# VectorE in source order inside each of the first 48 steps, weight conversion two chunks further ahead

## The chip, the cores and the metric

One core of a Trainium2 chip runs the whole program. The metric is the device time of one execution in microseconds (us), the median of three runs.

## What is computed

Three stages run one after the other on 1536 tokens (2 batches of 768) of width 512, all in float32 at the interface.

```
x = attention(q, k, v)          # 8 heads of 64; each query sees keys within 16 places,
                                # and the 24 block summaries (max of k, mean of v)
h = x @ w_in                    # 512 -> 2048
g = h * tanh(log1p(exp(h)))     # "mish"
x = g @ w_out                   # 2048 -> 512
out = x                         # then, where x @ w_skip > 0:
out += gate * relu(x @ w1[e]) @ w2[e]   # e = argmax of x @ w_gate, 8 experts of 512 -> 1024 -> 512
```

## The kernel before, in words

The change touches the middle stage, the two dense products around mish. Its tokens are cut into 4 blocks of 384 (`BLK`), its inner width of 2048 into 16 chunks f of 128. One **step** i is one pair (block n, chunk f), and there are 64 steps. Their order is the list `seq`: steps 0 to 9 are block 0 with f = 0 to 9, steps 10 to 25 are block 1 with f = 0 to 15, steps 26 to 31 finish block 0 with f = 10 to 15, and blocks 2 and 3 follow with 16 steps each. So the first 48 steps are blocks 0, 1 and 2.

Step i traces in the loop of `blocks()`, in this order:

- `m1` (L298): 12 matmuls on TensorE make h, the hidden chunk of 128 x 384, from the transposed tokens xt and the weights w. Each float32 operand is held as a high and a low part, so each product takes three matmuls. h lies in a pool of two PSUM buffers.
- `s1` (L311) on VectorE cuts h off at 20 and ScalarE (L312) takes exp.
- `s3` and `s4` of the step before: L331 and L335 on VectorE, then g is split in a high part on ScalarE (L339) and a low part on GpSimd (L340).
- `s2` and `s2b` of this step: L318 on VectorE, two activations on ScalarE (L319, L320), L326 on VectorE (the last reader of h), L327 on GpSimd.
- `more_w`: weight chunks are converted up to the number that `wneed` gives for this half step.
- the attention, loading and routing work that a table has set for half step 2i (`run_half`).
- `m2` of step i-2 (L369): 9 matmuls add g times the second weight into three PSUM tiles of 128 x 512.
- `more_w` and `run_half` again, for half step 2i+1.

In the texts m1(i), s1(i), s2(i), s2b(i), s3(i), s4(i) and m2(i) mean that function's work for step i. On VectorE s1, s2, s2b, s3 and s4 are one instruction each.

**Conversion.** The dense weights arrive as float64 words of 64 bits, in 32 chunks: chunk 2f holds the first weight of f, which m1 needs, chunk 2f+1 the second one, which m2 needs. `split_w` makes two float32 parts of one: three integer instructions on VectorE (L180, L182, L183), a copy on ScalarE (L186) that is the high part, and a subtraction on GpSimd (L187) that is the low one. Chunks 0 to 3 are converted in the start-up. After that `wneed(h)` says how many have to be done by half step h: h + 3 in the first 20 half steps, later one for every 2.5 half steps. Raw chunks are loaded `LA` = 6 chunks before their conversion.

**Attention** is cut in units of 128 queries by 4 heads, six to a block: units 0 to 5 for block 0 run in the start-up, units 6 to 11 for block 1 in steps 0 to 8. Each has four parts, `att_a` (scores, maximum, exp), `att_b` (transposes), `att_c` (product with v, division) and `att_d` (transposes on TensorE, L282; the high part of xt on ScalarE, L286; the low part on VectorE, L287). `AO[n]` gives the half steps of the four parts, counted from the unit's first. xt(u) is the VectorE instruction at L287 for unit u; m1(10), the first of block 1, needs xt(11).

**Order.** The program is traced in the order above, but the instructions of each engine are put in order by the tile framework, which picks among what is ready on a timeline of its own. `tc.manual_schedule` keeps the traced order for the engines that it is given. Before the change it stands around the start-up (SyncE alone) and around the expert stage (all engines); in the 64 steps every engine's order is picked.

```
def wneed(h):
    if h < 2 * FS:
        return h + 3
    return min(2 * NCH, max(2 * FS + 3, int(2 * FS + WC + (h - 2 * FS) * WD)))
```

Of the kernel before, what the change touches and what calls it, by code (L numbers as in the profile page):

```python
# [25 lines left out]
NCH = DFF // 128  # L26
# [14 lines left out]
WD = 0.4  # L41
AB = (0, 0, 42, 62)
AS = (0, 1.5, 2, 4)
AO = ((), (0, 3, 6, 8), (0, 5, 8, 11), (0, 5, 8, 11))
SH = 6
SI = 6
MPS = (6, 7, 8, 9, 10, 11)
# [4 lines left out]
GB = 5  # L52
XL = 2
LA = 6
LOADS = ("k0 q0 k1 c1 c0 q2 v0 q1 q4 v2 n1 n0 k2 v4 n2 v5 k3 q3 v3 q5 W4 v1").split()
STEPS = ("e0 e3 K0 x0 e2 z14 a0 e4 x4 w2 e1 K1 a4 x2 a2 z4 z8 b2 x3 V z8 x1 b0 y0 y4 b4 e5 c0 y2 c4 y5 c2 a1 "
         "a3 x5 d2 z4 y3 a5 d0 w1 d4 z4 y1 b1 b3 b5 c1 c3 c5 w4 d1 d3 w3 z4 d5").split()
# [3 lines left out]
def body(ctx: ExitStack, tc: tile.TileContext, a):  # L61
# [64 lines left out]
    def ones_v(t):  # L126
        for s in range(2):
            G.memset(t[96 * s:96 * s + 24, s, :, 64:65], 32.0)
# [162 lines left out]
    def m1(n, f):  # L291
        w = ring_t[f]
        x = xt[n]
        h = psh.tile([128, BLK], F32, tag="h", name="h")
        c = 0
        for k in range(4):
            for wi, xi in ((0, 0), (0, 1), (1, 0)):
                T.matmul(out=h, lhsT=w[wi][:, k * 128:(k + 1) * 128], rhs=x[:, xi, k, :],  # L298
                         start=(c == 0), stop=(c == 11))
                c += 1  # L300
        g_t[n, f] = [h]
# [3 lines left out]
    def s1(n, f, c=ALL):  # L305
        h = g_t[n, f][0]
        if c.start == 0:
            u = ep.tile([128, BLK], F32, tag="u", name="u")
            g_t[n, f] = [h, u, None, None, None]
        u = g_t[n, f][1]  # L310
        V.tensor_scalar(out=u[:, c], in0=h[:, c], scalar1=20.0, scalar2=None, op0=ALU.min)  # L311
        A.activation(out=u[:, c], in_=u[:, c], func=AF.Exp)  # L312
# [16 lines left out]
    def s3(n, f, c=ALL):  # L329
        h, u, nn = g_t[n, f][0:3]  # L330
        V.scalar_tensor_tensor(out=nn[:, c], in0=nn[:, c], scalar=2.0, in1=u[:, c], op0=ALU.add, op1=ALU.mult)  # L331
# [457 lines left out]
    def load_w(n):  # L789
        while wn[0] < min(n, 2 * NCH):  # L790
            f, c = wq[wn[0]]
            if f < NR:
                raw = ring.tile([128, 512], I64, tag="w", name="rawr")
            else:
                raw = stg.tile([128, 512], I64, tag="stg", name="raw")
            st["sp"] = nc.sync.dma_start(out=raw, in_=a["wio"][f, c]).ins
            st["w", f, c] = raw
            wn[0] += 1

    def more_w(n):  # L800
        while wn[1] < min(n, 2 * NCH):
            k = wn[1]
            load_w(min(k + LA - k % 2, 2 * NR) if k < 2 * NR - 1 else max(2 * NR, k + 2))
            split_w(*wq[k])
            wn[1] += 1
# [67 lines left out]
    def startup():  # L873
# [10 lines left out]
        for p in range(2):  # L884
            ones_v(vw[p])
        for x in LOADS:
            ITEMS[x[0]](int(x[1:]))
# [10 lines left out]
    def at_half(h, fn, x):  # L898
        half.setdefault(h, []).append((fn, x))

    seq = ([(0, f) for f in range(FS)] + [(1, f) for f in range(NCH)] + [(0, f) for f in range(FS, NCH)] +
           [(n, f) for n in range(2, NBLK) for f in range(NCH)])
    for n in range(1, NBLK):
        for x in range(6):
            u = 6 * n + x
            for o, fn in zip(AO[n], (att_a, att_b, att_c, att_d)):
                at_half(int(AB[n] + AS[n] * x) + o, fn, u)
# [30 lines left out]
    def run_half(h):  # L938
        for fn, x in half.pop(h, []):
            if fn in (kload, tri_load):  # L940
                with tc.issue_after(st["sp"]):
                    fn(x)
            else:
                fn(x)

    def wneed(h):
        if h < 2 * FS:
            return h + 3
        return min(2 * NCH, max(2 * FS + 3, int(2 * FS + WC + (h - 2 * FS) * WD)))

    rawp = gp = None

    def blocks():
        nonlocal rawp, gp
        last = len(seq) - 1
        for i in range(len(seq)):
            if i == 3 * NCH:
                att.close()
                rawp = ctx.enter_context(tc.tile_pool(name="rawp", bufs=4))
                gp = ctx.enter_context(tc.tile_pool(name="gp", bufs=2))  # L960
            m1(*seq[i])
            if i < last:
                s1(*seq[i])
            if i >= 1:
                s3(*seq[i - 1])
                s4(*seq[i - 1])
            if i < last:
                s2(*seq[i])
                s2b(*seq[i])
            more_w(wneed(2 * i))  # L970
            run_half(2 * i)
            if i >= 2:
                n, f = seq[i - 2]
                m2(n, f)
                if m2_ends(n, f)[1]:
                    for t in range(3):
                        if f == NCH - 1:
                            ev(3 * n + t)
                        else:
                            ev_part(t)  # L980
            more_w(wneed(2 * i + 1))
            if i >= 3 * NCH + 2:
                load_e(min(NRAW, 2 * (i - 3 * NCH)))
            run_half(2 * i + 1)
        cs = [slice(128 * t, 128 * t + 128) for t in range(3)]
        for t in range(3):
            for fn in (s1, s2, s2b, s3, s4):
# [128 lines left out]
```

## Time and profile before

| what | value |
|---|---|
| median of 3 runs | 594.76 us (594.69 to 595.54) |
| the profiled execution, its own time | 595.44 us |
| its span, first to last instruction | 593.5 us |
| TensorE busy | 522.0 us (88%) |
| VectorE busy | 428.7 us (72%) |
| ScalarE busy | 288.5 us (49%) |
| GpSimd busy | 300.7 us (51%) |
| mean granted TensorE clock | 0.970 |

The profiled execution took 595.44 us, 0.68 us more than the median; 1.9 us of it lie outside the span. All times in the rows are counted from the start of the span. In the profile's lines PE is TensorE's matmuls, PEld its weight loads, DVE VectorE, ACT ScalarE, POOL GpSimd, SP SyncE. A row of a timeline gives the start, the length, the engine, the line and what is written and read; "x12" after it means twelve instructions merged in one row; the bracket is the engine's idle time just before and what ended it. The share of busy time is a mean over stages with different limits, so stretches have to be read apart.

### The profile page before, as it was taken

To read this page: it belongs to the slowest core of one execution; us is meant where nothing else is said; L and a number is where in the kernel's file an instruction comes from. 1 tells how busy PE (TensorE), PEld (TensorE's weight loads), DVE (VectorE), ACT (ScalarE), POOL (GpSimd) and SP (SyncE) were. 2 spreads that over 40 slices of the span, in tenths; PEclk is the share of its full clock that TensorE was granted. 3 is DMA by queue.
4 is the path that set the end of the run, shared out by engine and by line. 5 is a ranking of instruction groups with operands and counts; after the bars stand their busy time and mean duration, and the time that the engine had idled before them with its cause. 6 is when DMAs were issued, how large, how long until landed. Compare 5 with 4: busy or idle time off the path is not lost. (4 is left out here: it accounts for less than half of the span.)

```text
span 593.5 us, 11154 instructions
## 1 busy us (share of the span) xinstructions
PE 522.0 (88%) x3870; PEld 424.1 (71%) x3870; DVE 428.7 (72%) x904; ACT 288.5 (49%) x602; POOL 300.7 (51%) x334
## 2 busy tenths in 40 slices
PE   4498798678999999999999999999879979598994
PEld 2266566567778888898888889888547857386883
DVE  2447999999998677677798896797587257466314
ACT  1545655445665446445444454434436247366322
POOL 3223365574787554436445454454457256666403
PEclk8599999979999999999999999999999999799999
DMA  8916444845320023250100317630229369891100
GB/s 263 334 33 236 150 150 159 283 152 177 111 61 28 7 55 122 76 180 19 48 14 2 142 48 276 222 129 1 107 81 353 140 230 397 300 359 49 35 19 15
DMA packets 40614, 82.57 MB, mean 139 GB/s; under 512 B 4749, under 2 KB 17297, under 8 KB 40536
## 3 DMA queue, kind: packets, MB, share of 16 engines
q1 hardware_dynamic: 38280, 75.03, 37.5%
q0 software_dynamic: 2256, 6.57, 3.5%
q8 instruction: 39, 0.64, 0.5%
q14 instruction: 39, 0.32, 0.2%
HBM read 72.92 MB, written 9.44 MB: 139 GB/s over the span
## 5 line engine op out<-in xcount | busy, mean ns | idle before, releaser
L298 PE MATMUL h<-xt,w 128*128 128x384 f32 x768 | 157.4, 347 | 10.3 <-DVE hn L326 5.1
L369 PE MATMUL o<-w,g 128*128 128x512 f32 x576 | 152.8, 404 | 7.6 <-ACT g L339 6.5
L298 PEld LDWEIGHTS h<-xt,w 128*128 128x128 f32 x768 | 134.1, 190 | 19.1 <-DVE hn L326 7.5
L369 PEld LDWEIGHTS o<-w,g 128*128 128x128 f32 x576 | 104.6, 189 | 32.8 <-ACT g L339 9.9
L327 POOL TENSOR_TENSOR hn<-hn,u 128x384 f32<-128x384 f32 (+1 forms) x66 | 79.8, 1209 | 81.7 <-ACT u L320 36.7
L340 POOL TENSOR_TENSOR g<-hn,g 128x384 fp32r<-128x384 f32 (+1 forms) x66 | 68.6, 1041 | 67.4 <-ACT g L339 63.7
L550 POOL TENSOR_TENSOR hl<-rawe,hl 128x128 fp32r<-128x128 f32 (+1 forms) x64 | 56.1, 902 | 17.7 <-ACT hl L546 17.0
L339 ACT ACTIVATE g<-hn 128x384 fp32r<-128x384 f32 (+1 forms) x66 | 33.9, 514 | 63.6 <-DVE hn L335 58.5
L319 ACT ACTIVATE u<-nn,two 128x384 f32<-128x384 f32 (+1 forms) x66 | 39.8, 604 | 47.6 <-DVE nn L318 47.6
L187 POOL TENSOR_TENSOR w<-r,w 128x512 fp32r<-128x512 f32 x32 | 44.1, 1382 | 30.1 <-ACT w L186 29.8
L335 DVE SCALAR_TENSOR_TENSOR hn<-nn,hn 128x384 f32<-128x384 f32 (+1 forms) x66 | 48.0, 729 | 14.9 <-POOL hn L327 14.7
L550 DVE TENSOR_TENSOR hl<-rawe,hl 128x384 fp32r<-128x384 f32 (+1 forms) x64 | 43.6, 719 | 17.5 <-ACT hl L546 15.8
L331 DVE SCALAR_TENSOR_TENSOR nn<-nn,u 128x384 f32<-128x384 f32 (+1 forms) x66 | 46.2, 701 | 13.2 <-ACT u L320 13.0
L318 DVE SCALAR_TENSOR_TENSOR nn<-u 128x384 f32<-128x384 f32 (+1 forms) x66 | 46.2, 700 | 12.0 <-ACT u L312 11.9
L312 ACT ACTIVATE u<-u 128x384 f32<-128x384 f32 (+1 forms) x66 | 33.9, 513 | 33.6 <-DVE u L311 32.0
L546 ACT ACTIVATE hl<-rawe 128x512 fp32r<-128x512 f32 (+1 forms) x64 | 43.1, 729 | 13.7 <-PEq L734 5.2
L585 PE MATMUL p<-hl,slx 128*128 128x512 f32 x168 | 41.7, 397 | 2.5 <-ACT slx L563 2.0
L602 PE MATMUL po<-hl,slh 128*128 128x512 f32 x168 | 43.1, 399 | 0.0
L585 PEld LDWEIGHTS p<-hl,slx 128*128 128x128 f32 x168 | 30.7, 188 | 9.4 <-ACT slx L563 2.7
L311 DVE TENSOR_SCALAR u<-h 128x384 f32<-128x384 f32 (+1 forms) x66 | 35.3, 535 | 2.6 <-PE h L298 2.6
L326 DVE TENSOR_TENSOR hn<-nn,h 128x384 f32<-128x384 f32 (+1 forms) x66 | 35.2, 534 | 1.4
L602 PEld LDWEIGHTS po<-hl,slh 128*128 128x128 f32 x168 | 30.6, 188 | 6.1
(173 smaller groups left out, 742.9 us busy)
## 6 DMA issues: line engine op xcount, KB each, us to landing
rawe<-w SPq DMA_DIRECT2D x64, 512.0 KB, 6.0
rawr<-wio SPq DMA_DIRECT2D x30, 512.0 KB, 5.1
vw<-vx SPq DMA_DIRECT2D x40, 97.5 KB, 2.1
xs<-x SPq DMA_DIRECT2D x12, 256.0 KB, 3.2
out<-x SPq DMA_DIRECT2D x12, 256.0 KB, 2.4
kw<-kx SPq DMA_DIRECT2D x18, 160.0 KB, 3.2
q<-qx SPq DMA_DIRECT2D x20, 128.0 KB, 2.8
kt<-kt SPq DMA_DIRECT2D x4, 384.0 KB, 4.9
```

What stands on the lines that cost most here:

```text
L187: G.tensor_tensor(out=w[1][:, o:o + 512], in0=r, in1=w[0][:, o:o + 512].bitcast(F32), op=ALU.subtract)
L298: T.matmul(out=h, lhsT=w[wi][:, k * 128:(k + 1) * 128], rhs=x[:, xi, k, :], start=(c == 0), stop=(c == 11))
L318: V.scalar_tensor_tensor(out=nn[:, c], in0=u[:, c], scalar=2.0, in1=u[:, c], op0=ALU.add, op1=ALU.mult)
L327: G.tensor_tensor(out=hn[:, c], in0=hn[:, c], in1=u[:, c], op=ALU.mult)
L331: V.scalar_tensor_tensor(out=nn[:, c], in0=nn[:, c], scalar=2.0, in1=u[:, c], op0=ALU.add, op1=ALU.mult)
L335: V.scalar_tensor_tensor(out=hn[:, c], in0=nn[:, c], scalar=2.0, in1=hn[:, c], op0=ALU.subtract, op1=ALU.mult)
L340: G.tensor_tensor(out=g[:, 1, c], in0=hn[:, c], in1=g[:, 0, c].bitcast(F32), op=ALU.subtract)
L369: T.matmul(out=o_t[t], lhsT=g[:, gi, t * 128:(t + 1) * 128], rhs=w[wi][:, 512:1024], start=(first and i == 0), stop=(end and i == 2))
L546: A.activation(out=w[0][:, c], in_=r[:, c], func=AF.Copy)
L550: eng.tensor_tensor(out=w[1][:, d], in0=r[:, d], in1=w[0][:, d].bitcast(F32), op=ALU.subtract)
L585: T.matmul(out=ps, lhsT=x[:, xi + k, :], rhs=w[wi][:, 512 * half:512 * half + 512], start=(k == 0 and xi == 0 and wi == 0), stop=(k == 3 a ...
L602: T.matmul(out=ps, lhsT=hs[f // 4][:, xi + f % 4, :], rhs=w[wi][:, 512 * (f % 2):512 * (f % 2) + 512], start=(f == 0 and i == 0), stop=(f ...
```

## The change

Three edits. `AO[1]` sets part d of units 6 to 11 one half step earlier (7 for 8). `wneed` asks for two more chunks in the first 20 half steps. And each of the first 48 steps runs inside a `manual_schedule` for VectorE. Lines of the code behind the insertion move down by one (L311 becomes L312), inside and behind the loop by more.

```
-AO = ((), (0, 3, 6, 8), (0, 5, 8, 11), (0, 5, 8, 11))
+AO = ((), (0, 3, 6, 7), (0, 5, 8, 11), (0, 5, 8, 11))
...
+MAN = {mybir.EngineType.DVE}
...
     def wneed(h):
         if h < 2 * FS:
-            return h + 3
+            return h + 5
...
-        for i in range(len(seq)):
+        def step(i):
+            nonlocal rawp, gp
             if i == 3 * NCH:
...
             run_half(2 * i + 1)
+
+        for i in range(len(seq)):
+            with (tc.manual_schedule(engines=MAN) if i < 3 * NCH else ExitStack()):
+                step(i)
```

What it does to the order of instructions shows in the lists of the two built programs. In the new VectorE list the instructions of one step stand in traced order, but each step has a context of its own, and those of two neighbouring steps are still mixed.

**VectorE, from the last instruction of the start-up into steps 0 and 1.** h, u, nn and hn are the tiles of s1, s2 and s2b; bits, r and rawr those of a chunk's conversion; mx and psc belong to att_a. Before:

```order
L287 TENSOR_TENSOR xt_487<-psx_642,xt_487 128x2x128
L180 TENSOR_SCALAR bits_748<-rawr_258 128x512
L182 SCALAR_TENSOR_TENSOR bits_748<-rawr_258,bits_748 128x512
L214 TENSOR_REDUCE mx_683<-psc_672 128x4
L183 SCALAR_TENSOR_TENSOR r_749<-rawr_258,bits_748 128x512
L215 TENSOR_SCALAR mx_683<-mx_683 128x4
L180 TENSOR_SCALAR bits_755<-rawr_260 128x512
L182 SCALAR_TENSOR_TENSOR bits_755<-rawr_260,bits_755 128x512
L183 SCALAR_TENSOR_TENSOR r_756<-rawr_260,bits_755 128x512
L311 TENSOR_SCALAR u_662<-h_649 128x384
```

With the change:

```order
L288 TENSOR_TENSOR xt_487<-psx_642,xt_487 128x2x128
L312 TENSOR_SCALAR u_664<-h_651 128x384
L312 TENSOR_SCALAR u_752<-h_739 128x384
L319 SCALAR_TENSOR_TENSOR nn_667<-u_664 128x384
L327 TENSOR_TENSOR hn_671<-nn_667,h_651 128x384
L181 TENSOR_SCALAR bits_680<-rawr_258 128x512
L183 SCALAR_TENSOR_TENSOR bits_680<-rawr_258,bits_680 128x512
L332 SCALAR_TENSOR_TENSOR nn_667<-nn_667,u_664 128x384
L184 SCALAR_TENSOR_TENSOR r_681<-rawr_258,bits_680 128x512
```

Before, chunks 4 and 5 and one maximum of att_a stand ahead of s1(0). Now s1(0) and s1(1) stand first, and chunk 4 follows s2b(0).

**VectorE, the ten instructions that end with s4(9).** ksum and sl belong to the key summaries of the second batch. s4(9) is the last row of both lists. Before:

```order
L182 SCALAR_TENSOR_TENSOR bits_1736<-rawr_1445,bits_1736 128x512
L180 TENSOR_SCALAR bits_1794<-rawr_1447 128x512
L326 TENSOR_TENSOR hn_1442<-nn_1438,h_1417 128x384
L156 TENSOR_REDUCE ksum10_105<-sl_1638 128x24
L318 SCALAR_TENSOR_TENSOR nn_1495<-u_1487 128x384
L156 TENSOR_REDUCE ksum10_105<-sl_1650 128x24
L182 SCALAR_TENSOR_TENSOR bits_1794<-rawr_1447,bits_1794 128x512
L331 SCALAR_TENSOR_TENSOR nn_1438<-nn_1438,u_1430 128x384
L326 TENSOR_TENSOR hn_1499<-nn_1495,h_1474 128x384
L335 SCALAR_TENSOR_TENSOR hn_1442<-nn_1438,hn_1442 128x384
```

With the change:

```order
L319 SCALAR_TENSOR_TENSOR nn_1487<-u_1479 128x384
L184 SCALAR_TENSOR_TENSOR r_1441<-rawr_1272,bits_1440 128x512
L181 TENSOR_SCALAR bits_1456<-rawr_1274 128x512
L327 TENSOR_TENSOR hn_1491<-nn_1487,h_1466 128x384
L181 TENSOR_SCALAR bits_1500<-rawr_1369 128x512
L183 SCALAR_TENSOR_TENSOR bits_1456<-rawr_1274,bits_1456 128x512
L332 SCALAR_TENSOR_TENSOR nn_1487<-nn_1487,u_1479 128x384
L183 SCALAR_TENSOR_TENSOR bits_1500<-rawr_1369,bits_1500 128x512
L184 SCALAR_TENSOR_TENSOR r_1457<-rawr_1274,bits_1456 128x512
L336 SCALAR_TENSOR_TENSOR hn_1491<-nn_1487,hn_1491 128x384
```

In the first piece pieces of chunks 24 and 25, two summaries, s2(10) and s2b(10) stand ahead of s4(9). In the second it is chunks 20, 21 and 22, and no summary and nothing of step 10. Counted from the top of the list, s4(9) is instruction 203 of VectorE before and 192 now. The eleven that have gone behind it are L180 and L182 of chunks 23, 24 and 25, L183 of chunk 22, two summaries (L156), s2(10) and s2b(10). Nothing has come ahead of it.

**VectorE and TensorE around xt(11), with the change.** xn_1336 is unit 11's attention output, psx_1382 its transpose. VectorE:

```order
L336 SCALAR_TENSOR_TENSOR hn_1366<-nn_1362,hn_1366 128x384
L319 SCALAR_TENSOR_TENSOR nn_1427<-u_1419 128x384
L184 SCALAR_TENSOR_TENSOR r_1376<-rawr_1179,bits_1375 128x512
L263 RECIPROCAL rs_1333<-rs_1333 128x4
L327 TENSOR_TENSOR hn_1431<-nn_1427,h_1406 128x384
L272 TENSOR_TENSOR xn_1336<-psv_1322,rs_1333 128x256
L288 TENSOR_TENSOR xt_1010<-psx_1382,xt_1010 128x2x128
```

TensorE, the last three of the nine matmuls of m2(7), two of m1(9), six of m1(10) and the transpose:

```order
L370 MATMUL o_887<-w0_1183,g_1424 128x512
L370 MATMUL o_888<-w0_1183,g_1424 128x512
L370 MATMUL o_889<-w0_1183,g_1424 128x512
L299 MATMUL h_1466<-xt_487,w0_1373 128x384 x2
L299 MATMUL h_1526<-xt_1010,w0_262 128x384 x2
L299 MATMUL h_1526<-xt_1010,w1_263 128x384
L299 MATMUL h_1526<-xt_1010,w0_262 128x384 x2
L299 MATMUL h_1526<-xt_1010,w1_263 128x384
L283 MATMUL psx_1382<-cb_94,xn_1336 128x128 x2
```

Before, xn(11) and xt(11) have four other VectorE instructions between them, and on TensorE the transpose follows m1(7). Now xt(11) stands directly behind xn(11), and the transpose behind m2(7), two matmuls of m1(9) and six of m1(10).

## Rows read from the trace of the kernel before

**Rows 1.** Stretches: length, then PE, PEld, DVE, ACT, POOL busy, clock, DMA share, GB/s.

```profile
45.00:60.00 15.00, 12.36 (x126) 9.04 (x126) 11.28 (x26) 7.57 (x23) 4.25 (x4) 1.00 0.68 243
60.00:105.00 45.00, 37.45 (x287) 28.40 (x288) 43.69 (x84) 26.96 (x64) 25.27 (x21) 1.00 0.49 151
105.00:135.00 30.00, 21.52 (x102) 17.29 (x102) 30.00 (x57) 13.74 (x26) 19.15 (x16) 0.89 0.58 207
135.00:150.00 15.00, 12.78 (x72) 11.03 (x74) 13.89 (x22) 8.07 (x18) 7.78 (x8) 1.00 0.58 176
150.00:200.00 50.00, 49.03 (x328) 39.79 (x321) 46.53 (x80) 29.96 (x61) 36.49 (x31) 1.00 0.21 61
200.00:250.00 50.00, 50.00 (x344) 43.36 (x342) 35.93 (x73) 27.44 (x55) 25.48 (x22) 1.00 0.25 72
```

**Rows 2.** VectorE's lines in 54.5 to 138 us: busy us, mean ns, idle before.

```profile
L182 DVE SCALAR_TENSOR_TENSOR bits<-rawr,bits 128x512 int32<-128x512 int32 x22 | 15.0, 683 | 0.1
L180 DVE TENSOR_SCALAR bits<-rawr 128x512 int32<-128x512 int32 x22 | 14.9, 683 | 1.1 <-ACT sc L217 0.6 <-ACT at L245 0.4
L183 DVE SCALAR_TENSOR_TENSOR r<-rawr,bits 128x512 int32<-128x512 int32 x19 | 12.8, 676 | 0.1
L318 DVE SCALAR_TENSOR_TENSOR nn<-u 128x384 f32<-128x384 f32 x11 | 9.0, 822 | 0.1
L335 DVE SCALAR_TENSOR_TENSOR hn<-nn,hn 128x384 f32<-128x384 f32 x9 | 8.3, 926 | 0.1
...
L326 DVE TENSOR_TENSOR hn<-nn,h 128x384 f32<-128x384 f32 x11 | 6.0, 541 | 0.0
...
L156 DVE TENSOR_REDUCE ksum<-sl 128x24 f32<-128x768 f32 x2 | 1.9, 940 | 0.0
```

**Rows 3.** Timeline of TensorE and VectorE at the end of the start-up.

```profile
53.98 0.96 PE L298 MATMUL h<-xt,w 128*128 128x384 f32 x4
...
54.10 0.42 DVE L287 TENSOR_TENSOR xt<-psx,xt 128x256 fp32r<-128x256 f32 x1 [0.97 <-ACT xt L286]
...
57.99 1.33 PE L298 MATMUL h<-xt,w 128*128 128x384 f32 x6
...
59.31 0.55 DVE L311 TENSOR_SCALAR u<-h 128x384 f32<-128x384 f32 x1
```

**Rows 4.** Timeline of 111 to 122 us, all engines.

```profile
111.77 0.41 PE L282 MATMUL psx<-cb,xn 128*128 128x128 f32 x2 [1.14 <-DVE xn L271]
...
112.22 0.39 ACT L286 ACTIVATE xt<-psx 128x256 fp32r<-128x256 f32 x1 [0.37 <-PE psx L282]
...
120.27 0.68 DVE L180 TENSOR_SCALAR bits<-rawr 128x512 int32<-128x512 int32 x1
...
120.86 0.67 DVE L183 SCALAR_TENSOR_TENSOR r<-rawr,bits 128x512 int32<-128x512 int32 x1
...
121.53 3.57 PE L298 MATMUL h<-xt,w 128*128 128x384 f32 x10 [2.08 <-POOL w L187]
```

**Rows 5.** The view of Rows 1, one short stretch.

```profile
120.00:125.00 5.00, 3.47 (x11) 3.48 (x12) 5.00 (x8) 2.18 (x4) 3.15 (x3) 0.55 0.39 148
```

**Rows 6.** Timeline from s4(9) to m1(15), TensorE, ScalarE, GpSimd and VectorE.

```profile
138.03 0.55 DVE L335 SCALAR_TENSOR_TENSOR hn<-nn,hn 128x384 f32<-128x384 f32 x1
...
138.67 0.53 ACT L339 ACTIVATE g<-hn 128x384 fp32r<-128x384 f32 x1 [1.48 <-DVE hn L335]
...
139.42 1.02 POOL L340 TENSOR_TENSOR g<-hn,g 128x384 fp32r<-128x384 f32 x1
...
143.33 2.35 PE L369 MATMUL o<-w,g 128*128 128x512 f32 x9 [0.70 <-ACT x L352]
...
145.52 4.35 PE L298 MATMUL h<-xt,w 128*128 128x384 f32 x24
...
149.80 0.85 PE L138 MATMUL psv<-vl,strip 128*24 128x128 f32 x22
...
157.26 4.45 PE L298 MATMUL h<-xt,w 128*128 128x384 f32 x24
```

## Prediction

> **What bounds the kernel now.** I first read the busy time of each engine by stretches [rows 1], because the shares over the whole span mix stages with different limits. From 200 us on TensorE is busy 50.00 us of 50 and VectorE only 35.9: there the order of VectorE's instructions can cost something, but it can hardly gain. Between 60 and 135 us it is the other way round. VectorE is busy 43.69 of 45 and 30.00 of 30 us, and TensorE loses 7.6 us in the first of these stretches and 8.5 in the second; from 135 to 150 us it loses 2.2, from 150 to 200 us 1.0. So VectorE sets the pace in steps 0 to about 11, and TensorE from about step 13 to the end of the dense stage. A better order can give back at most what TensorE lost there.
>
> Next I read what VectorE does in its own stretch [rows 2]. Of its time, 15.0, 14.9 and 12.8 us go into conversion, and there is hardly an idle moment: 1.1 us ahead of L180, ended by ScalarE. A conversion instruction of 0.68 us starts 0.59 us after the one before it [rows 4], so one costs some 0.08 us less than its mean length says. With that, L180, L182 and L183 cost 0.60 each, s2 0.74, s2b 0.47, a summary (L156) 0.86.
>
> So the question is what stands in VectorE's list ahead of the instructions that TensorE waits for. The best mark is s4(9), which starts at 138.03 us [rows 6]: with it m2(9) becomes possible, and soon after TensorE works without a gap to speak of.
>
> **What leaves the place ahead of s4(9).** By the lists, s4(9) is VectorE's instruction 203 before and 192 now. Eleven have gone behind it: seven of conversion (7 x 0.60 = 4.2 us), two summaries (1.7), s2(10) and s2b(10) (1.2). Nothing has come ahead of it. That is **-7.1 us**, as long as VectorE stays busy. The two more chunks of the new `wneed` are no load here: before, the planner had run even further ahead, into chunk 25, by itself. What is moved costs the same later: ahead of s4(17) the new list is 23 instructions shorter, ahead of s4(25) only four, and from 150 us on TensorE sets the pace. Chunk 31 now stands just ahead of s4(25), whose m2(25) is the first to need it.
>
> **What it costs in waiting.** VectorE works strictly along its list. Where conversion used to fill a wait, now there may be nothing.
>
> - *Start.* xt(5) ends at 54.52 us [rows 3]. Before, chunks 4 and 5 and a maximum follow at once and s1(0) comes at 59.31. Now s1(0) and s1(1) follow, and s1(1) needs the end of m1(1). Of m1(0) and m1(1) twelve matmuls are left by then, at 0.18 us each (24 in 4.35 us) [rows 6], so 2.2 us and a little for the last to end: s1(1) starts at about 57.0. Less the 0.5 us of s1(0), VectorE idles **2.0 us**.
> - *xt(11).* It now stands directly behind xn(11), and its transpose stands on TensorE behind m2(7) and eight matmuls of m1. From the end of s4(7): high part of g 0.53 and low part 1.02 [rows 6], of m2(7) then seven matmuls at 0.26 (9 in 2.35 us) 1.8, eight at 0.18 1.4, the transposes 0.41 and ScalarE's part 0.39 [rows 4]: 5.6 us. VectorE meanwhile has s2(8), one L183, s2b(8), a reciprocal and xn(11). The last two, which have no row here, I put at 0.5 together by their few columns; in all 2.3 us. So it waits **3.3 us**, and s1(9) and all behind it wait too.
> - *s1(5) and s1(8).* Here the new TensorE list has six matmuls of m2(i-2) inside m1(i), so s1(i) closes a ring: s4(i-2), both parts of g (1.55), four m2 (1.0), ten m1 (1.8), 4.4 us. VectorE has by the prices above about 4.2 and 4.0 us of work in between: **0.6 us** in all. At the other steps the ring has a microsecond or more of room.
>
> Together 5.9 us, so s4(9) comes 1.2 us earlier and ends at 137.4.
>
> **From there to the end.** TensorE gets the high part of g(9) at 138.0. From there to m1(15) its new list holds m1(12), m1(13), m1(14) (36 x 0.18 = 6.5 us) and m2(9), m2(10), m2(11) with six matmuls of m2(12) (33 x 0.26 = 8.6): 15.1 us, and I add 1.0 us for places where it still waits for s4(10) and s2b(11), which gain less than s4(9). m1(15) then starts at 154.1. Before, it starts at 157.26 [rows 6], with three matmuls of m2(12) (0.8) and 24 small ones of the value summaries (22 take 0.85) [rows 6] more behind it, so the like point is 155.6. The gain is 1.5 us. The 1.1 us that VectorE idled ahead of L180 [rows 2] was a conversion standing in line for a PSUM buffer that an exp of att_a still read. Now conversion and attention follow each other as traced, and I take it as gained, with a little for the row's waits behind it: **-2.7 us** in all. From m1(15) on TensorE has the same work as before and is full; routing and the later attention are moved by some places on VectorE, under TensorE's 50.00 of 50, and I cost that at nothing. If this cover fails, it costs what s4 comes late, in steps 40 to 43 above all, where 26 small routing instructions stand in two steps.
>
> The other two edits go into the same lists: `AO` moves xt(6) to xt(11) half a step earlier in the traced order, and the raw chunks are loaded six chunks ahead as before. In rows 2 no conversion waits for a load, so I cost the loads at nothing, between nothing and the 0.6 us of one instruction.
>
> The sum is made against the profiled execution (595.44 us, which is 0.68 above the median); I set it on the median: 594.76 - 2.7 = **592.0 us**. The bounds of this case itself: the start wait is at best 1.4 us (s1(0) filled in) and the wait at xt(11) is halved if the low part of g comes early, which gives 2.5 us more, 589.5; with no gain from the 1.1 us and each wait half as long again, 594.6.
>
> **Rivals.**
>
> *A, the waits don't come.* The whole 7.1 us arrive, and 1.0 that TensorE lost after 150 us: 586.7 us. For it: TensorE loses 19 us from 60 to 150 us, so there is room [rows 1]. Against it: the lists show the wait at xt(11) plainly.
>
> *B, the clock.* Before, the granted clock falls to a mean of 0.55 between 120 and 125 us [rows 5], a mix of 2.4 and 1.2 GHz, after TensorE had stood still for 2.08 us ahead of m1(9) [rows 4]; ten of that step's matmuls then took 3.57 us, 1.8 more than at 0.18 each. That was hidden behind VectorE. Now m1(9) and m1(10) stand ahead of xt(11), so it would be seen: 593.8 us. Against it: with attention and m2 spread more evenly, TensorE's gaps should be shorter. The Trainium skill (TensorE: Matmul & The Clock Gate, What's actually happening) says that a gate sets the array's clock by how busy it has lately been; by that rule the wait at xt(11), in which TensorE is working, would not bring the fall, and the gap ahead of m1(9) would.
>
> *C, slower: VectorE stands in line.* In the old list a late operand held up one instruction, and conversion ran on. In the new one all of s3, s4, s2 stand behind it, and TensorE behind them. The place is the ring at s1(5), s1(8) and xt(11), with under half a microsecond of room at the first two. It runs through GpSimd's low part of g, and GpSimd also makes the low part of each chunk, for which TensorE stood 2.08 us before m1(9) [rows 4]. If it comes in between at all three, 6.2 us are lost: 594.76 - 2.7 + 6.2 = 598.3 us. It decides from two such delays on. For it: s1(5) and s1(8) have no slack. Against it: GpSimd is busy only 25.3 of 45 us [rows 1].
>
> A price that also belongs here: s2 and s4 take 822 and 926 ns while s2b, with as many elements, takes 541 [rows 2]. If the ten s2 of steps 0 to 9 came to s4's price, 1.0 us would be lost, which stays inside the range. The Trainium skill (GPSIMD Engine Reference, Specifications) says that GpSimd shares its SBUF interfaces with VectorE and that instructions with two SBUF inputs contend; s2 and s4 read two from SBUF, s2b one, so the rows agree. By that rule s2, s3 and s4, which now stand closer together, could meet GpSimd more often.
>
> That the change does nothing is excluded by the lists; that it keeps a single traced order is not what it does, since two steps are still mixed.
>
> **How the numbers follow.** The forecast has 0.48, A 0.18, B 0.14, C 0.20. A measurement of this kernel can tell about 0.2% from no change, 1.2 us. The forecast is faster by more than that in about six parts of seven, A always, B in a third, C never, with a mild form near zero: **faster 0.63, same 0.19, slower 0.18**. The range that leaves out 0.2 reaches to A on one side and to a C with one and a half of its three delays on the other (592.0 + 3.1, and the contention's 1.0): **586.5 to 596.2**. The forecast's own is 589.5 to 594.6.
>
> **What would show it.** Right: VectorE idle for about 2 us at 55 to 57 us, by m1, and 3 us ahead of an L288 near 121 us; s4(9) between 135 and 138 us and no L157 ahead of it; TensorE's lost time from 105 to 150 us down from 10.7 to about 7 us, and a clock near 1.00 from 120 to 135. Wrong: idle time of VectorE ahead of L312 that adds up to over 8 us (C), a clock under 0.9 there (B), a wait at xt(11) under 1 us (A), or TensorE under 49 us in 50 after 200 us, by which the cost that I put at nothing would be real.

## The result, and the profile after

The changed kernel takes **603.09 us** (median of 4 runs, 601.01 to 607.12) against 594.73 us (4 runs, 594.35 to 595.54) of the kernel before: 1.0136 times as long, with a 95% interval of 1.0100 to 1.0173. It is slower by about 8 us, where 592.0 us was predicted with a range of 586.5 to 596.2. The profiled execution took 603.09 us, its span is 601.2 us, the mean granted clock 0.956. Executions more than 1.5% above the fastest one of their kernel are left out of every ratio below.

The stretches after, in the columns of [rows 1]: length, then busy time of PE, PEld, DVE, ACT and POOL, clock, DMA share, GB/s.

```profile
60.00:105.00 45.00, 37.06 (x262) 28.77 (x262) 43.41 (x78) 25.47 (x60) 23.97 (x21) 0.92 0.54 167
105.00:135.00 30.00, 21.42 (x136) 17.43 (x135) 25.35 (x51) 12.10 (x24) 13.68 (x12) 0.94 0.55 191
135.00:150.00 15.00, 11.27 (x44) 8.84 (x44) 14.69 (x22) 7.50 (x15) 11.31 (x10) 0.89 0.24 78
150.00:200.00 50.00, 48.50 (x289) 41.90 (x289) 44.48 (x78) 27.43 (x61) 30.96 (x28) 1.00 0.29 90
200.00:250.00 50.00, 48.69 (x374) 41.50 (x373) 42.14 (x82) 28.29 (x57) 29.31 (x27) 1.00 0.30 87
250.00:300.00 50.00, 50.00 (x369) 44.30 (x368) 31.83 (x71) 24.36 (x48) 21.15 (x20) 1.00 0.26 79
350.00:400.00 50.00, 47.56 (x247) 42.99 (x246) 39.69 (x101) 22.04 (x43) 21.81 (x19) 0.93 0.58 191
```

From 105 to 135 us VectorE has 4.65 us in which it does nothing, where before it had none [rows 1], and TensorE is busy no longer for it (21.42 us, before 21.52). From 200 to 250 us TensorE loses 1.3 us, which it did not before.

Two kinds of loss show in VectorE's lines from 55.5 to 142.2 us, the stretch that answers to [rows 2]: busy us, mean ns, idle before.

```profile
L183 DVE SCALAR_TENSOR_TENSOR bits<-rawr,bits 128x512 int32<-128x512 int32 x19 | 12.9, 687 | 0.2
L181 DVE TENSOR_SCALAR bits<-rawr 128x512 int32<-128x512 int32 x19 | 12.7, 682 | 0.0
L184 DVE SCALAR_TENSOR_TENSOR r<-rawr,bits 128x512 int32<-128x512 int32 x18 | 12.1, 679 | 0.2
L319 DVE SCALAR_TENSOR_TENSOR nn<-u 128x384 f32<-128x384 f32 x10 | 8.6, 864 | 0.2 <-ACT u L313 0.2
L336 DVE SCALAR_TENSOR_TENSOR hn<-nn,hn 128x384 f32<-128x384 f32 x9 | 8.5, 940 | 0.1
L332 DVE SCALAR_TENSOR_TENSOR nn<-nn,u 128x384 f32<-128x384 f32 x10 | 8.3, 830 | 0.0
L312 DVE TENSOR_SCALAR u<-h 128x384 f32<-128x384 f32 x11 | 6.1, 552 | 3.0 <-PE h L299 3.0
...
L288 DVE TENSOR_TENSOR xt<-psx,xt 128x256 fp32r<-128x256 f32 x7 | 2.9, 418 | 4.9 <-ACT xt L287 4.9
```

The line of s3 before, which [rows 2] leaves out:

```profile
L331 DVE SCALAR_TENSOR_TENSOR nn<-nn,u 128x384 f32<-128x384 f32 x10 | 7.1, 714 | 0.0
```

Conversion is there in the expected smaller number. But s2, s3 and s4 (L319, L332, L336) are no cheaper in sum, 25.4 us for 29 instructions where it was 24.4 for 30. And of the 7.9 us of idle time ahead of L312 and L288, 6.9 are new; 0.97 stand ahead of xt(5), as before ([rows 3]).

The second place lies at 351 to 362 us (timeline; the bracket is idle time and its releaser):

```profile
351.43 0.26 DVE L479 TENSOR_TENSOR so<-oh,oj 128x104 fp32r<-128x104 bf16 x1
...
353.55 1.62 DVE L487 TENSOR_SCALAR so<-cb,pm,val 128x128 fp32r<-128x128 f32 x6
...
355.09 0.55 DVE L332 SCALAR_TENSOR_TENSOR nn<-nn,u 128x384 f32<-128x384 f32 x1
...
355.56 0.54 DVE L312 TENSOR_SCALAR u<-h 128x384 f32<-128x384 f32 x1
...
357.70 0.54 DVE L327 TENSOR_TENSOR hn<-nn,h 128x384 f32<-128x384 f32 x1
...
358.30 4.21 PE L299 MATMUL h<-xt,w 128*128 128x384 f32 x12 [2.44 <-DVE hn L327]
```

Twelve routing instructions of block 1 (L479, L482, L487), from 351.43 to 355.1 us, stand ahead of s3(48) and s1(49). s2b(49) comes late, m1(51) waits 2.44 us for the PSUM buffer that it reads, and then runs at the lower clock level, 1.2 GHz: twelve matmuls in 4.21 us, 0.35 each, where one took 0.18 before [rows 6].

To see where it accumulates I take **TensorE's lag**: each matmul counts its kind's median step in the trace of before, and the lag is the difference of the times at which both traces have done the same sum. It is 1.0 us at 50 us (the start-up of this execution is that much longer), 4.7 at 80 to 100, 5.3 at 190 and 230, 6.2 at 310, 5.0 at 340, and 7.9 to 8.7 from 360 on. So two thirds are lost up to 190 us and most of the rest by 360 us. Between 100 and 220 us the two traces have TensorE's work in another order, and there the lag depends by several us on how the small matmuls are counted. The dense steps themselves catch up for a while: s4(17), with 23 instructions less ahead of it, starts at 181.13 us, before at 181.80, and s4(30), when these have been made up, at 250.73, before at 243.48.

### The profile page after: what moved, and what is told of

It reads as the page before. It is cut to its first block, busy times and chain, and to the rows that moved or that the text cites. A ratio compares the mean times of both kernels' runs of the same rounds, so it can differ in the third digit from the quotient of the medians.

```text
span 601.2 us, 11116 instructions
## 1 busy us (share of the span) xinstructions
PE 523.0 (87%) x3867; PEld 427.4 (71%) x3870; DVE 429.5 (71%) x904; ACT 287.9 (48%) x602; POOL 290.8 (48%) x334
## 5 line engine op out<-in xcount | busy, mean ns | idle before, releaser
L370 PE MATMUL o<-w,g 128*128 128x512 f32 x576 | 156.8, 409 | 15.8 <-ACT g L340 15.8
L299 PEld LDWEIGHTS h<-xt,w 128*128 128x128 f32 x768 | 136.7, 192 | 15.5 <-DVE hn L327 4.9
L370 PEld LDWEIGHTS o<-w,g 128*128 128x128 f32 x576 | 106.7, 193 | 40.8 <-ACT g L340 21.3
L341 POOL TENSOR_TENSOR g<-hn,g 128x384 fp32r<-128x384 f32 (+1 forms) x66 | 67.9, 1030 | 102.9 <-ACT g L340 102.9
L328 POOL TENSOR_TENSOR hn<-hn,u 128x384 f32<-128x384 f32 (+1 forms) x66 | 73.4, 1113 | 37.5 <-ACT u L321 31.4
L188 POOL TENSOR_TENSOR w<-r,w 128x512 fp32r<-128x512 f32 x32 | 42.0, 1315 | 51.1 <-ACT w L187 48.4
L332 DVE SCALAR_TENSOR_TENSOR nn<-nn,u 128x384 f32<-128x384 f32 (+1 forms) x66 | 47.1, 713 | 9.5 <-ACT u L321 9.2
L336 DVE SCALAR_TENSOR_TENSOR hn<-nn,hn 128x384 f32<-128x384 f32 (+1 forms) x66 | 44.6, 676 | 12.9 <-POOL hn L328 10.9
L319 DVE SCALAR_TENSOR_TENSOR nn<-u 128x384 f32<-128x384 f32 (+1 forms) x66 | 43.1, 653 | 5.5 <-ACT u L313 5.5
L312 DVE TENSOR_SCALAR u<-h 128x384 f32<-128x384 f32 (+1 forms) x66 | 35.5, 538 | 15.0 <-PE h L299 14.9
L327 DVE TENSOR_TENSOR hn<-nn,h 128x384 f32<-128x384 f32 (+1 forms) x66 | 35.3, 535 | 1.3
```

The lines of the kernel that those rows point to most:

```text
L188: G.tensor_tensor(out=w[1][:, o:o + 512], in0=r, in1=w[0][:, o:o + 512].bitcast(F32), op=ALU.subtract)
L319: V.scalar_tensor_tensor(out=nn[:, c], in0=u[:, c], scalar=2.0, in1=u[:, c], op0=ALU.add, op1=ALU.mult)
L328: G.tensor_tensor(out=hn[:, c], in0=hn[:, c], in1=u[:, c], op=ALU.mult)
L336: V.scalar_tensor_tensor(out=hn[:, c], in0=nn[:, c], scalar=2.0, in1=hn[:, c], op0=ALU.subtract, op1=ALU.mult)
L341: G.tensor_tensor(out=g[:, 1, c], in0=hn[:, c], in1=g[:, 0, c].bitcast(F32), op=ALU.subtract)
L370: T.matmul(out=o_t[t], lhsT=g[:, gi, t * 128:(t + 1) * 128], rhs=w[wi][:, 512:1024], start=(first and i == 0), stop=(end and i == 2))
```

## Experiments

The runs are numbered 1 to 12. Where the source order is taken away, the framework picks VectorE's order again; it is called the planner below. Each run is compared with runs of the kernel before on the same chip; the ratio has a 95% interval, mostly of 0.3% to each side (1.8 us). The diffs are against the changed kernel. A second measure comes from the trace alone: the time from the end of xt(5), the last VectorE instruction of the start-up, to the start of s4(9), split into VectorE's idle time and the rest, its work (I add up the idle times ahead of all instructions between the two). "Longer" is what s2, s3 and s4 there, s4(9) included, last in sum above 545 ns each, their length when nothing disturbs them. Each row is one profiled execution. The changed kernel, run 2 and run 7 have the same order there and agree within 0.1 us; run 5, which has it too, is 2.9 us longer, so a smaller difference between two rows is not firm.

| run | ratio to before | xt(5) to s4(9) | idle | work | longer |
|---|---|---|---|---|---|
| before | 1 | 83.5 | 1.5 | 82.0 | 8.2 |
| changed | 1.0136 | 86.7 | 7.9 | 78.8 | 9.6 |
| 5, changed, again | 1.0143 | 89.6 | 9.8 | 79.9 | 10.5 |
| 1, no source order | 1.0005 | 84.4 | 2.8 | 81.6 | 9.3 |
| 2, source order 0 to 25 | 1.0069 | 86.7 | 7.8 | 78.8 | 9.6 |
| 3, 26 to 47 | 1.0013 | 84.3 | 1.9 | 82.4 | 8.3 |
| 4, 10 to 25 | 1.0009 | 83.6 | 4.9 | 78.7 | 10.1 |
| 6, 0 to 9 | 1.0223 | 87.8 | 8.2 | 79.6 | 10.0 |
| 7, 0 to 43 | 1.0094 | 86.7 | 7.8 | 78.8 | 9.6 |
| 8, 0 to 25, both fills | 0.9955 | 80.4 | 6.1 | 74.2 | 4.1 |
| 9, 0 to 25, late xt | 0.9974 | 82.5 | 3.6 | 78.9 | 8.1 |
| 10, 0 to 25, start filled | 0.9985 | 80.5 | 7.2 | 73.4 | 4.3 |
| 11, 0 to 47, both fills | 1.0009 | 82.0 | 7.2 | 74.8 | 5.8 |
| 12, 0 to 25, more fill | 0.9980 | 83.2 | 4.7 | 78.6 | 9.0 |

**1. Which of the three edits.** The source order goes, the other two edits stay:

```diff
-            with (tc.manual_schedule(engines=MAN) if i < 3 * NCH else ExitStack()):
+            with (ExitStack()):
```

> The changed kernel without the source order on VectorE; the earlier part d of units 6 to 11 and the two more chunks in wneed stay. Theory 1 (the loss of 8.4 us is all due to the source order: about 5.3 us in steps 0 to 13 and about 3.5 near 350 us): as before the change, 593.5 to 596. Rival (the two small edits cost it, because they put more conversion ahead of the attention): 600 or more.

Measured: 1.0005 (0.9971 to 1.0039). The conversion further ahead and the earlier part d cost nothing that can be measured without the source order; with it, the loss comes. Whether the source order alone, without these two edits, costs as much in steps 0 to 25 was not run.

**2. Steps 0 to 25 only.** The condition becomes `if i < FS + NCH`.

> The changed kernel with the source order in steps 0 to 25 only; steps 26 to 47 are ordered by the planner again. Theory 1 (two separate losses): the loss near 350 us goes and the first one stays, 599.5 (598.5 to 600.5). Rival 2 (the second loss is the first one handed on, a block that starts 5 us late meets its routing late): 602 to 604. Rival 3 (all is lost in the first 13 steps and regained or lost again by chance later): no forecast, but TensorE's lag in the trace at 340 us and at 400 us would be unlike.

Measured: 1.0069 (1.0037 to 1.0100), 4.1 us. TensorE's lag stays at 2.6 to 2.9 us from 210 to 410 us, 4.5 above its -1.8 at 50 us: the first loss is there, the second one isn't.

**3. Steps 26 to 47 only**, without the two small edits:

```diff
-            return h + 5
+            return h + 3
...
-            with (tc.manual_schedule(engines=MAN) if i < 3 * NCH else ExitStack()):
+            with (tc.manual_schedule(engines=MAN) if FS + NCH <= i < 3 * NCH else ExitStack()):
```

(`AO[1]` is that of before as well.)

> The kernel before with the source order in steps 26 to 47 only, without the two small edits. Theory 1: only the loss near 350 us, 594.7 + 3.5 = 598.2 (597 to 599.5), and the trace is the one of before up to 240 us. Rival 2 (the second loss follows from the first): 594 to 596.

Measured: 1.0013 (0.9981 to 1.0045), 0.8 us with nearly 2 to each side: less than expected, and alone no proof. Its trace has the second place just as the changed kernel has, though this block comes early (view of the waits, TensorE, 330 to 375 us: total us, times, longest):

```profile
PE h L299 <- DVE hn L327: 2.5, 1, 2.5
```

In the traces of runs 2 and 8, without source order from step 26 on, this wait is 0.6 us, as before the change. The lag grows from -1.4 us at 250 us to 0.2 to 0.4 at 400 to 420 us: 1.7 us. I had put it at 3.5, from the step of the curve at 350 us alone; but the kernel before loses 0.7 us of its own between 300 and 340 us, which the source order saves (40.00 of 40 us busy, before 39.30), and that has to be set against it.

**4. Steps 10 to 25 only.** The condition becomes `if FS <= i < FS + NCH`.

> The changed kernel with the source order in steps 10 to 25 only. Theory 1 with the loss in steps 0 to 9 (start, the ring at s1(8), the wait for xt(11), longer s2 and s3): 594.5 to 596. Rival 4 (the loss comes behind step 9, where conversion of the later chunks stands ahead of s4): 598 to 600.

Measured: 1.0009 (0.9977 to 1.0040). From 200 to 250 us TensorE is busy 48.69 us, as in the changed kernel, where the run without source order has 50.00. So the 1.3 us lost there come from steps 10 to 25; since the time as a whole is no longer, they are won back elsewhere, where is not shown.

**5. The changed kernel again**, beside the next three on one chip.

> The changed kernel itself once more, so that it stands beside the parts on one chip. All theories: 1.010 to 1.017 of the kernel before. In its trace TensorE lags behind the kernel before by 3.5 to 5.5 us from 180 to 340 us and by 2 to 4 us more from 360 us on; if the second step isn't there again, it was an accident of one profile.

Measured: 1.0143 (1.0094 to 1.0193). The lag is 6.2 to 7.5 us from 180 to 250 us, more than expected, and 8.5 to 8.8 from 400 to 420, less of a second step. One program, two executions: the table shows 2.9 us between them before s4(9). The largest single difference at one place that remains at the end, 1.57 us, is this one. In the changed kernel's first profile, the chain to xt(11) is (timeline):

```profile
124.75 0.55 DVE L336 SCALAR_TENSOR_TENSOR hn<-nn,hn 128x384 f32<-128x384 f32 x1
...
125.90 2.33 PE L370 MATMUL o<-w,g 128*128 128x512 f32 x9 [1.39 <-ACT g L340]
...
128.07 1.58 PE L299 MATMUL h<-xt,w 128*128 128x384 f32 x8
...
129.49 0.38 PE L283 MATMUL psx<-cb,xn 128*128 128x128 f32 x2
...
129.91 0.39 ACT L287 ACTIVATE xt<-psx 128x256 fp32r<-128x256 f32 x1 [2.46 <-PE psx L283]
...
130.32 0.42 DVE L288 TENSOR_TENSOR xt<-psx,xt 128x256 fp32r<-128x256 f32 x1 [3.10 <-ACT xt L287]
```

and in this one (timeline, and the stretch in the columns of [rows 1]):

```profile
124.68 3.92 PE L370 MATMUL o<-w,g 128*128 128x512 f32 x9 [3.25 <-ACT g L340]
...
130.66 0.42 DVE L288 TENSOR_TENSOR xt<-psx,xt 128x256 fp32r<-128x256 f32 x1 [4.67 <-ACT xt L287]
```

```profile
125.00:130.00 5.00, 5.00 (x20) 4.16 (x18) 1.00 (x4) 1.21 (x3) 2.96 (x3) 0.67 1.00 401
```

The nine matmuls of m2(7) take 3.92 us instead of 2.33, after TensorE had stood still for 3.25 us; the granted clock of these 5 us is 0.67, a mix of 2.4 and 1.2 GHz. VectorE waits in line for them, and so its wait is 1.57 us longer (4.67 for 3.10).

**6. Steps 0 to 9 only.** The condition becomes `if i < FS`.

> The changed kernel with the source order in steps 0 to 9 only. Theory 1 (the first loss arises in steps 0 to 9): the same loss as with steps 0 to 25, 1.004 to 1.010 of the kernel before. Rival (it takes the source order on both sides of step 10, so that what is late in step 9 isn't made good behind it): 1.000 to 1.003.

Measured: 1.0223 (1.0184 to 1.0261), worse than the whole change, which nobody had forecast. Up to s4(9) it is like the others; the lag jumps from 1.6 us at 140 to 11.4 at 150. VectorE's lines from 138 to 160 us say why:

```profile
L157 DVE TENSOR_REDUCE ksum<-sl 128x24 f32<-128x768 f32 x4 | 3.8, 938 | 0.0
L183 DVE SCALAR_TENSOR_TENSOR bits<-rawr,bits 128x512 int32<-128x512 int32 x5 | 3.4, 681 | 0.0
L184 DVE SCALAR_TENSOR_TENSOR r<-rawr,bits 128x512 int32<-128x512 int32 x5 | 3.4, 674 | 0.0
```

With four L181 more that is 9.5 us of conversion and 3.8 us of summaries in 22 us; s4(11) starts at 158.7 us, in the run with steps 0 to 25 at 150.7. What the source order keeps back in steps 0 to 9, the planner puts ahead of s3 and s4 as soon as it may. With the source order in steps 10 to 25 as well (run 2) this doesn't happen.

**7. Steps 0 to 43 only.** The condition becomes `if i < 44`.

> The changed kernel with the source order in steps 0 to 43 only. Theory (the second loss is the routing of block 1 that the source order holds back in steps 46 and 47, until it meets s3(48) and s1(49)): only the first loss stays, 1.005 to 1.009, and m1(51) doesn't wait for hn. Rival (the loss is spread over steps 26 to 47, or starts with the routing in step 40): 1.010 or more.

Measured: 1.0094 (1.0058 to 1.0130), between the two. m1(51) doesn't wait for hn, as expected, but the lag still grows by 2.0 us from 250 us on (3.6 to 5.6 at 400): now TensorE waits twice for g, 1.5 us ahead of m2(46), with other routing instructions between s3(46) and s4(46), and 0.8 us ahead of m2(47), behind nine routing instructions (L482, L487) between s2(47) and s2b(47), which start 3.5 us apart instead of 1.5 before the change. So the second loss isn't the end of the source order alone; in what way the source order in the steps before leads to it is open.

**8. VectorE's waits filled**, source order in steps 0 to 25 (as in 2). Chunk 4 is traced ahead of s1(0), and the low part of xt(6) to xt(11) one step later:

```diff
             m1(*seq[i])
+            if i == 0:
+                more_w(wneed(0))
             if i < last:
                 s1(*seq[i])
...
                 s2b(*seq[i])
+            while late:
+                late.pop()(0)
             more_w(wneed(2 * i))
...
-        V.tensor_tensor(out=xt[n][:, 1, 2 * p:2 * p + 2, o:o + 128], in0=ps, in1=hi.bitcast(F32), op=ALU.subtract)
...
+        def low(_):
+            V.tensor_tensor(out=xt[n][:, 1, 2 * p:2 * p + 2, o:o + 128], in0=ps, in1=hi.bitcast(F32), op=ALU.subtract)
+        if n == 1:
+            late.append(low)
+        else:
+            low(0)
```

> The changed kernel with the source order in steps 0 to 25, with two edits that put work into VectorE's waits: chunk 4 is traced ahead of s1(0), and the low part of xt(6) to xt(11) is traced behind s2b of the step after, so that a chunk stands ahead of xt(11). Theory 2 (the first loss is VectorE's waits in line: 3.1 us for xt(11), 1.9 for two more xt, 3.0 for s1): VectorE idle between 54 and 150 us falls from 8.8 to 3 us or less and the time to 0.999 to 1.003 of the kernel before. Rival 5 (the first loss is s2 and s3 getting longer beside GpSimd, and TensorE's wait for g, which this doesn't touch): 1.005 or more, with the idle time moved to TensorE or to other lines.

Measured: **0.9955** (0.9924 to 0.9986): faster than the changed kernel by some 11 us, and with no loss left against the kernel before. That it is 2.7 us faster than the kernel before isn't secure: one execution of 586.52 us, 4.9 below the next, weighs much in this ratio, and the median of all twelve is 594.49 us against 595.17 (0.9989). Theory 2 isn't borne out as it was put: the idle time fell only from 7.8 to 6.1 us, while the work fell from 78.8 to 74.2. The waits for xt are gone, others have come (1.9 us for a maximum of att_a), and s2, s3 and s4 got shorter. Both theories have a part, so the fills were taken apart.

**9. The late xt alone** (the second and third piece of that diff).

> The changed kernel with the source order in steps 0 to 25 and only one of the two fills: the low part of xt(6) to xt(11) is traced behind s2b of the step after. Theory 2: of the waits only those for xt go, 0.87 and 3.1 us in the trace of the changed kernel; from 1.0069 (source order in steps 0 to 25) to 0.999 to 1.002 of the kernel before, and s1 in the start still waits. Rival 6 (the fill of the start is what helped): 1.005 or more.

Measured: 0.9974 (0.9946 to 1.0003). This separates the waits: the work is all but the same (78.9 us), the idle time 3.6 instead of 7.8. Between 54 and 150 us the waits that are left are (VectorE: total, times, longest):

```profile
DVE u L319 <- PE h L306: 2.2, 2, 1.9
DVE hn L343 <- POOL hn L335: 0.9, 1, 0.9
DVE nn L339 <- ACT u L328: 0.6, 1, 0.6
```

xt is missing, and of the waits for h only those in the start, at s1(0) and s1(1), are left. 4.2 us of stretch and 0.95% of time (5.6 us) against run 2.

**10. The start alone** (the first piece).

> The same with the other fill only: chunk 4 is traced ahead of s1(0). Theory 2: only the waits of the start go, 1.5 us, and the list behind it moves a little; 1.003 to 1.006, and xt(11) still waits 3 us or more. Rival 6: 0.995 to 1.000.

Measured: 0.9985 (0.9956 to 1.0015), more than the theory gave it, and xt(11) doesn't wait, against the expectation: the first edit also shifts how neighbouring steps are mixed, and xt(11) now stands behind s1(8) and s3(7). The idle time is 7.2 us all the same (4.0 for h), and s1(0), which the edit was to help, still waits 1.12 us. This run separates the other part: the work falls by 5.4 us. From 52 to 133.9 us:

```profile
L336 DVE SCALAR_TENSOR_TENSOR hn<-nn,hn 128x384 f32<-128x384 f32 x10 | 8.3, 830 | 0.5 <-POOL hn L328 0.3
L319 DVE SCALAR_TENSOR_TENSOR nn<-u 128x384 f32<-128x384 f32 x10 | 6.5, 655 | 0.0
...
L332 DVE SCALAR_TENSOR_TENSOR nn<-nn,u 128x384 f32<-128x384 f32 x10 | 5.8, 579 | 0.0
```

The same thirty instructions last 20.6 us where they lasted 25.9 in the changed kernel; what has changed is their place against GpSimd's work (last section).

**11. The source order in steps 26 to 47, beside both fills** (the condition as in the changed kernel).

> The changed kernel (source order in steps 0 to 47) with both fills. Theory 3 (the source order in steps 26 to 47 costs about 2 us by itself, wherever the routing of block 1 lands): 0.9955 + 0.003 = 0.996 to 1.001 of the kernel before; TensorE's lag against the run with both fills grows by 1 to 3 us between 250 and 400 us. Rival 7 (that loss is there only where the block comes late): 0.9955, no growth.

Measured: 1.0009 (0.9982 to 1.0036). Against run 8 that is 0.54% more, and the wait of m1(51) for hn is there with 2.5 us; the lag grows from -3.8 us at 250 us to -2.4 at 400. Theory 3 agrees by the trace; by the times it is not firm, since the two intervals overlap a little and run 8's ratio is the uncertain one.

**12. More filling.** Chunk 5 also ahead of s1(0), and the chunks of step 3 ahead of s1(3):

```diff
+            if i in (0, 3):
+                more_w(wneed(2 * i + (i == 0)))
```

in place of the first piece in 8.

> Source order in steps 0 to 25 and both fills, and more filling: chunk 5 also ahead of s1(0), and the chunks of step 3 ahead of s1(3), where VectorE still waited 1.5 us for h in the run with both fills. Theory 2 taken further: VectorE idle from 54 to 150 us falls by 2 us or more, 0.991 to 0.995 of the kernel before. Rival 8 (what stands ahead of s1 now delays TensorE more than the filled wait is worth): 0.996 or more.

Measured: 0.9980 (0.9955 to 1.0005), as rival 8 had it and not theory 2. Idle time falls to 4.7 us, but s2, s3 and s4 meet GpSimd again (9.0 us longer) and the stretch is 83.2 us. So an emptier list of waits is not the aim by itself. That this is slower than run 8 isn't settled, the intervals overlap.

## Why the prediction was wrong

By the lag, the 8 us come together like this, against the steps of the prediction.

**The step that failed first is "-7.1 us, as long as VectorE stays busy".** Eleven instructions did leave the place ahead of s4(9) (153 to 142 between xt(5) and s4(9)), but VectorE's work there fell by 3.2 us, not 7.1. The prices of conversion held but for 0.02 us each (56 instructions, 0.9 us). s2, s3 and s4 cost 2.0 us more than priced, and the six scalings of the maxima in att_a (L216) 1.0. The prediction priced these instructions at their mean in the trace of before and put the risk at 1.0 us. But their length isn't a property of the instruction: it is 0.545 us, or longer until GpSimd's running instruction has ended (last section), and so it belongs to the order. Runs 9 and 10 show that it can be 24.5 or 20.6 us for the same thirty.

**The waits were right in kind and place, and nearly right in sum.** Foreseen were +5.9 us and 1.1 back; measured is 1.5 idle before and 7.9 after. The start: 1.23 and 0.31 us ahead of s1(0) and s1(1), predicted 2.0. xt(11): 3.10 us, predicted 3.3, from a chain of 5.0 us (the rows in experiment 5), predicted 5.6. s1(8): 1.44, where 0.6 was predicted for s1(5) and s1(8) together and s1(5) waits 0.05. Not foreseen were 0.87 us at xt(7). That the sum comes so near is partly luck: two terms were too large and two too small. Run 9 shows that without the waits for xt and s1(8) nothing is left of the loss in steps 0 to 25.

With -3.2 and +6.3 us, and 1.0 us of a longer start-up in this execution, s4(9) starts at 142.2 us, 4.2 later than before; predicted was 1.2 earlier. The predicted sign hung on a difference of two nearly equal terms, 7.1 and 5.9, of which one was half wrong.

**"From there to the end" failed too.** Another 1.5 us were to be gained behind s4(9); instead the lag at 230 us is 5.3, 1.1 more than s4(9) was late. This is m2(8) in the changed kernel (timeline):

```profile
135.78 3.89 PE L370 MATMUL o<-w,g 128*128 128x512 f32 x9 [3.11 <-ACT g L340]
```

It waits 3.11 us for g, and its nine matmuls take 3.89 us, at 1.2 GHz for much of it, instead of 2.35 [rows 6]. This is rival B in another place: TensorE's lower clock is hidden no longer where VectorE waits for TensorE in line, and run 5 shows that it moves the same program by 1.57 us at xt(11) alone. TensorE does work through the wait at xt(11), as the prediction said; the clock fell after the standstill just ahead of it, before m2(7), in the execution where that lasted 3.25 us, and not in the one where it lasted 1.39. The clock is not the whole of the loss, though: from 54 to 150 us the mean granted clock is 0.96 in the kernel before and 0.93 in the changed one, but also 0.95 in runs 2 and 7, which lose, 0.89 in runs 3 and 4, which don't lose measurably, and 0.93 in run 8. Then come the 1.3 us between 200 and 250 us, where m1 waits for a conversion that the source order makes just in time (L187 and L188, 0.6 and 0.7 us at 210 to 212 us) and that the planner had done long before (the low part starts at 210.7 us, before at 175.1).

**"Cost at nothing" for the later steps was wrong**, by about 2 us: 2.7 by the lag of the first profile from 250 us on, 1.3 in run 5, 1.7 in run 3, 1.4 in run 11. By the times it would be some 4 us (1.0136 against run 2's 1.0069, two intervals that touch), so the size is open. "From 200 us on TensorE is busy 50.00 us of 50" was read from one stretch, 200 to 250 us. In the kernel before, the stretch with the routing of blocks 0 and 1 is not full, and VectorE is busy 43.62 us in it, not 35.93 (columns of [rows 1]):

```profile
300.00:350.00 50.00, 48.59 (x309) 42.39 (x309) 43.62 (x118) 21.55 (x44) 23.80 (x21) 1.00 0.13 47
```

And where TensorE is full, it is covered only as far as two PSUM buffers of h reach: routing of 3.7 us in one piece ahead of s1 is longer than it lasts. The prediction had named the danger (what s4 comes late) and placed it at steps 40 to 43; it came at 47 to 49, and through s2b rather than s4.

**The tell-tales.** Right: idle time of 1.5 us at 55 to 58 us and 3.1 us ahead of an L288, though at 130 and not 121 us. Wrong: s4(9), TensorE's loss from 105 to 150 us (12.3 us instead of 10.7 before, predicted 7), and the clock from 120 to 135 us (0.93 instead of 1.00). The last one named, TensorE under 49 us in 50 after 200 us, came true twice (48.69 and 47.56), but it was true before the change too (48.59, above), so it could not tell. **Rival C** had the sign and the places, but its mechanism came in halves: the waits ahead of L312 are 3.0 us in all, and GpSimd did its harm through the length of s2, s3 and s4 more than through its part of the ring.

**Sums.** The prediction's own bounds don't come out of its terms: 592.0 with no gain from the 1.1 us and half of 5.9 more is 596.1, not 594.6, and its better case gives 2.25 us (0.6 and half of 3.3), not 2.5. From 60 to 150 us TensorE loses 18.3 us, not 19. None of this reaches 603.

What stays open: whether any of the fills makes the kernel faster than the one before, and which is best, since runs 8, 9, 10 and 12 don't separate; and how much of the second loss is the wait of m1(51) and how much what the steps before it lead to (run 7).

## What to carry to other kernels

An order kept as written puts every instruction in line behind the latest operand ahead of it; before switching it on, walk along the list for places where two waiting instructions stand together with nothing between them, and move ready work (here a conversion, or the waiting instruction itself by one step) into that place. Don't price the gain of a shorter list at the mean lengths of a trace when the lengths depend on what another engine does at that moment: price the undisturbed length, and count the meetings apart. And a change whose forecast is the difference of two terms of equal size is a forecast of no sign.

## What the runs showed of the hardware

**s2, s3 and s4 wait for GpSimd's instruction to end.** From 62.7 us, changed kernel (timeline):

```profile
62.72 1.42 POOL L188 TENSOR_TENSOR w<-r,w 128x512 fp32r<-128x512 f32 x1 [1.75 <-ACT w L187]
62.93 1.62 DVE L319 SCALAR_TENSOR_TENSOR nn<-u 128x384 f32<-128x384 f32 x1
...
64.10 1.31 POOL L341 TENSOR_TENSOR g<-hn,g 128x384 fp32r<-128x384 f32 x1
...
64.48 0.97 DVE L216 TENSOR_SCALAR mx<-mx 128x4 f32<-128x4 f32 x1
```

s2 starts 0.21 us after L188 and ends at 64.55, 0.41 us after it. That is a rule here: between xt(5) and s4(9) of the changed kernel, s4(9) included, all 11 of the s2, s3 and s4 that started while a GpSimd instruction was running ended 0.412 to 0.417 us after that one; the 19 others took 0.55. From 54 to 400 us in the kernel before there are 76 such meetings, with quartiles of 0.413 and 0.418; one of them is not held up (0.55 us). So a meeting costs what is left of GpSimd's instruction less 0.13 us, at most about 1.1 beside an L188. GpSimd's spans, which are rough, point the other way too: in the same stretch of the kernel before, the 41 L327 on GpSimd that started while s2, s3 or s4 ran took 1.33 us in the median, the 18 others 1.02. s1, s2b and conversion, which have a PSUM operand, show nothing of it (s2b 0.54 in either case). The 16-byte scaling L216, SBUF to SBUF with one input, does: 0.15 us alone, 0.97 here, ending 0.03 us after L341.

The Trainium skill (SBUF — State Buffer, 🔬 SBUF: two separate sides) says that VectorE and GpSimd share a port pair that is an exclusive lock for whole instructions, which VectorE's instructions with two SBUF inputs (against a GpSimd instruction that reads SBUF, as L188, L328 and L341 do) or in a two-port mode have to take. The rows agree: the VectorE instruction that is held up ends at one fixed time, 0.41 us, behind the end of GpSimd's. The prediction named only that the two contend; with the lock the 8.2 us in the trace of before could have been read as what they are, a matter of the order.

**The lower clock comes and goes between executions of one program.** m2(7) took 2.33 us at 2.4 GHz in one and 3.92, at 1.2 GHz for the most part, in the other (experiment 5), both after TensorE had waited, 1.39 and 3.25 us. In a stretch where VectorE leads and TensorE's gaps are hidden, nobody sees this; an order that lets VectorE wait for TensorE adds it to the time.
